# First loads on two DMA queues, biases spread by TensorE, batch 1's first stage from step 2, and matmuls on zeros, in a Fourier and mixture-of-experts kernel

## The chip, the core and the metric

One Trainium2 chip, of which the kernel uses one core. The metric is the device time of one execution in microseconds (us); three runs of the kernel before are given. Engines are named as in the profile: PE is TensorE (matmul), PEld its weight load, DVE VectorE, ACT ScalarE, POOL GpSimd, SP SyncE, which here issues DMAs only.

## The reference

Eight batches of x, each 3136 x 256, float32. Per batch: a real FFT along the 3136 rows, a complex matrix product with w_r + i w_i plus biases, a soft threshold (0.01) on real and imaginary part, and the inverse FFT. On its result `a`, a gate score per row picks 128 rows, which go through a two-layer network and are added back:

```python
X = np.fft.rfft(x, axis=1); Xr, Xi = X.real, X.imag
Yr = Xr @ w_r - Xi @ w_i + b_r
Yi = Xr @ w_i + Xi @ w_r + b_i
Yr = np.sign(Yr) * np.maximum(np.abs(Yr) - 0.01, 0)   # Yi likewise
a = np.fft.irfft(Yr + 1j * Yi, n=3136, axis=1)
scores = np.einsum('bsd,d->bs', a, w_gate)
for b in range(8):
    top = np.argpartition(-scores[b], 128)[:128]
    xe = a[b, top]
    out[b, top] = xe + sigmoid(scores[b, top])[:, None] * (np.maximum(xe @ w1, 0) @ w2)
```

## The kernel before, in words

The transform of 3136 = 98 x 32 rows is done in two stages each way, all as matmuls against tables. Batch by batch:

- **s1** (first stage, 16 units of two columns per batch, U = 16). `ld_x` loads x in tiles of four columns (98 x 1024, 392 KB), eight per batch. For batch 0, `s1` is one float32 matmul per unit on the tile as loaded, against `w1f`. From batch 1 on, `split_x` first splits the tile into a high and a low part (ACT writes `xh`, POOL subtracts for `xl`) and `mm3` makes three matmuls. The result goes from PSUM (four "s" buffers) to SBUF by ACT for even and DVE for odd units, and per two units a tile of 392 KB is stored to a scratch in DRAM, `As`.
- **s2** (13 groups per batch, G = 13). `ld_a` loads `As` back transposed (`av`, 512 KB, two groups per load); four matmuls against `g_sb` give `px` (one PSUM buffer), which ACT, DVE and POOL split into `Xh` and `Xl`.
- **spectral**: 24 matmuls per group with the split weights wrh, wrl, wih, wil into `py`; then DVE adds `bias`, ACT and DVE apply the threshold, and ACT and DVE split into `Yh`, `Yl`.
- **s2i**: six matmuls per group against `gip` (POOL's own queue brings that table in seven pieces); ACT copies the result out, DVE takes the gate's dot product with `wgb`, and it goes to a scratch `Cs`.
- **s1i** and the expert network follow 17 and more steps later and are not touched.

The main loop runs over steps t. In step t stand s2 of group t+1, spectral of group t and s2i of group t-1. Batch 0's first stage stands in the steps before 0; batch 1's has a schedule of its own (lines 595 to 603): loads from t = -2, splits from -1, s1 from 0, spread over ten steps. From batch 2 on it runs 16 steps ahead of the group it serves. `consts_a` (weights and biases) is called before the loop, `consts_g` and `consts_gi` in single steps. The order in which the program's calls reach an engine is settled by a scheduler when it is built; each engine then takes its instructions strictly in that order. `queued` keeps the loads of one queue (`ld` on SP, `ld_r` on POOL) in the order of the program. DMAs of SP and ACT take eight semaphores in turn, so that a DMA isn't issued before the eighth one ahead of it has landed.

Of the kernel before, what the change touches and what calls it, by code (L numbers as in the profile page):

```python
# [10 lines left out]
F32 = mybir.dt.float32  # L11
# [11 lines left out]
NF = 64  # L23
LAM = 0.01
# [84 lines left out]
def fourier_moe(ctx: ExitStack, tc: tile.TileContext, x, w_r, w_i, b_r, b_i, wg, w1, w2,  # L109
# [57 lines left out]
    def consts_a():  # L167
        for src, h, l in ((w_r, wrh, wrl), (w_i, wih, wil)):
            t = pool.tile([128, 2, D], F32, name="r1" if l is wrl else "Yl", bufs=1 if l is wrl else YB)
            ld(t, src.rearrange("(h p) e -> p h e", p=128))  # L170
            nc.vector.tensor_copy(h, t)
            nc.vector.tensor_tensor(out=l, in0=t, in1=h.bitcast(F32), op=ALU.subtract)
        for c, src in enumerate((b_r, b_i)):
            ld(bias[c * NF:(c + 1) * NF], src.rearrange("(o a e) -> o a e", o=1, a=1).broadcast_to([NF, 2, D]))
        nc.vector.tensor_scalar(out=bias, in0=bias, scalar1=LAM, scalar2=None, op0=ALU.add)
        nc.vector.memset(m2l, -2.0 * LAM)
# [5 lines left out]
    def consts_gi(k):  # L182
        s = slice(4 * k, min(4 * k + 4, NJ))
        ld_r(gip[:, s], t_gi[:, s])
        if k == 0:
            ld(wgb, wg.rearrange("(o e) -> o e", o=1).broadcast_to([128, D]))

# [182 lines left out]
    def width(g):  # L370
        return 1 if g == G - 1 else 2

    def ld_x(b, i):
        if i % 2 == 0:
            xt[b, i] = xt[b, i + 1] = pool.tile([N1, 4, D], F32, name=("xt", "cv", "av")[i // 2 // 3] if b == 0 else "xt", bufs=2 if b == 0 and i >= 12 else 3)
            ld(xt[b, i], xv[b, :, 2 * i:2 * i + 4, :])

# [203 lines left out]
    for i in range(U):  # L581
        ld_x(0, i)
    consts_a()
    consts_g(0)
    for t in range(-LEAD, B * G + LAG + 1):
# [3 lines left out]
        if t + LEAD < G or t + LEAD >= 2 * G:  # L589
            at_step(t + LEAD, s1, U)  # L590
        if t == -2:
            ld_x(1, 0)
            consts_g(1)
        at_step(t + AP, ld_a, G)
        for i in range(U):
            if t == -2 + i * 10 // U and i:
                ld_x(1, i)
            if t == -1 + i * 10 // U:
                split_x(1, i)
                if i == 0:  # L600
                    consts_gi(0)
            if t == i * 10 // U:
                s1(1, i)
        if t + LEAD + XP >= 2 * G:
            at_step(t + LEAD + XP, ld_x, U)
# [47 lines left out]
```

## Time and profile before

| | us |
|---|---|
| median of 3 runs (lowest, highest) | 766.38 (764.88, 767.89) |
| the profiled execution's own time | 765.34 |
| its span, first to last instruction | 763.5 |
| PE busy in the span | 727.8 (95%) |
| DVE, ACT, POOL busy | 520.4, 488.3, 356.1 |
| chain that ended last: PE, DVE, DMA | 80%, 9%, 6% |

The span is what the trace shows; the execution's own time has 1.8 us more around it. PE is busy nearly everywhere but in the first 60 us and the last 50. The chain that ended last is read from the end back to what released each piece; its DMA share lies almost wholly at the beginning and at the end.

### The profile page before, as it was taken

Reading aid. Unit: us, or ns where it says so; the run is one execution under the profiler, and the core shown is the slowest. Engines: PE = TensorE matmul, PEld = TensorE weight load, DVE = VectorE, ACT = ScalarE, POOL = GpSimd, SP = SyncE. Lnnn points to the kernel's source line nnn. Section 1 sums busy time; section 2 is a strip of 40 time slices with the busy share of each in tenths; the row PEclk is TensorE's granted clock in tenths of the full one; section 3 lists DMA queues with packets and bytes.
Section 4 is the critical chain, followed back from the end, with each engine's and each line's share of the span. In section 5 each row is a group of like instructions: output and inputs, shape, how many; then the busy total and the mean of one; then the engine's idle time right before and its main releaser. Section 6 shows DMA issues by size and latency. Waiting matters only on the chain.

```text
span 763.5 us, 14877 instructions
## 1 busy us (share of the span) xinstructions
PE 727.8 (95%) x5194; PEld 648.0 (85%) x5194; DVE 520.4 (68%) x1406; ACT 488.3 (64%) x994; POOL 356.1 (47%) x371
## 2 busy tenths in 40 slices
PE   6489999999999999999999999999999999999987
PEld 2279999998999899999998888888999888888657
DVE  2247766666566656655898898676687799887652
ACT  2246666778777767778778768677576565555331
POOL 0154545556666755556455555565453323233011
PEclk9699999999999999999999999999999999999998
DMA  8888958788887887687777778677574374343740
GB/s 225 303 250 270 292 190 279 253 249 277 258 258 236 270 246 250 210 269 242 242 232 234 228 207 263 203 237 215 166 225 146 124 220 140 109 132 113 243 148 22
DMA packets 86650, 165.59 MB, mean 217 GB/s; under 512 B 6413, under 2 KB 59182, under 8 KB 86574
## 3 DMA queue, kind: packets, MB, share of 16 engines
q1 hardware_dynamic: 84302, 158.99, 67.0%
q0 software_dynamic: 2160, 5.60, 2.5%
q8 instruction: 41, 0.67, 0.4%
q14 instruction: 35, 0.29, 0.1%
q10 hardware_dynamic: 112, 0.04, 0.0%
HBM read 86.56 MB, written 78.12 MB: 216 GB/s over the span
## 4 chain that ended last, share of the span: by engine, by line
PE 80%; DVE 9%; DMA 6%; issue 3%; ACT 1%; POOL 0%; SPq 0%; POOLq 0%; ACTq 0%; DVEq 0%
PE py L221 11%; PE py L223 11%; PE py L222 11%; PE px L418 10%; PE s L223 9%; PE s L221 9%; PE s L222 9%; DMA xt<-in_x 2%; PE m L346 2%; DMA As<-at 2%; PE s L501 1%; PE s L393 1%; PE py L346 1%; DVE w L265 1%; DVE Yl L217 1%
## 5 line engine op out<-in xcount | busy, mean ns | idle before, releaser
L217 POOL TENSOR_TENSOR cl<-cv,ch 98x512 fp32r<-98x512 f32 x112 | 144.3, 1290 | 188.0 <-ACT ch L215 131.2
L217 POOL TENSOR_TENSOR xl<-xt,xh 98x512 fp32r<-98x512 f32 x112 | 144.5, 1292 | 126.4 <-ACT xh L215 115.8
L459 ACT COPY ct<-s 128x512 f32<-128x512 f32 (+1 forms) x104 | 59.3, 570 | 164.3 <-PE s L223 150.6
L221 PE MATMUL py<-wrh,Xh 128*128 128x256 f32 x400 | 121.6, 304 | 0.0
L418 PEld LDWEIGHTS px<-g_sb,av 128*128 128x128 f32 (+1 forms) x800 | 106.7, 194 | 13.0 <-DVE Csc L463 1.2
L223 PE MATMUL py<-wrl,Xh 128*128 128x256 f32 x400 | 113.2, 283 | 0.0
L221 PE MATMUL py<-wih,Xh 128*128 128x256 f32 x400 | 113.0, 283 | 0.0
L222 PE MATMUL py<-wih,Xl 128*128 128x256 f32 x400 | 112.9, 282 | 0.0
L223 PE MATMUL py<-wil,Xh 128*128 128x256 f32 x400 | 112.7, 282 | 0.0
L222 PE MATMUL py<-wrh,Xl 128*128 128x256 f32 x400 | 112.7, 282 | 0.0
L463 DVE CUSTOM_DVE_ANT_0 junk<-s,wgb 128x256 f32<-128x256 f32 (+1 forms) x200 | 84.3, 421 | 38.6 <-ACT ct L459 35.3
L418 PE MATMUL px<-g_sb,av 128*128 128x128 f32 (+1 forms) x800 | 109.3, 279 | 0.0
L217 DVE TENSOR_TENSOR Yl<-py,Yh 128x512 fp32r<-128x512 f32 (+1 forms) x104 | 69.3, 666 | 45.4 <-ACT Yh L215 45.4
L438 DVE TENSOR_TENSOR py<-py,bias 128x512 f32<-128x512 f32 (+1 forms) x104 | 70.2, 675 | 42.8 <-PE py L223 42.6
L423 DVE TENSOR_TENSOR Xl<-px,Xh 128x512 fp32r<-128x512 f32 (+1 forms) x104 | 69.2, 666 | 19.6 <-ACT Xh L422 13.2
L215 ACT CAST xh<-xt 98x512 fp32r<-98x512 f32 x112 | 72.3, 651 | 16.0 <-DMA xt<-in_x 14.3
L221 PEld LDWEIGHTS py<-wrh,Xh 128*128 128x128 f32 x400 | 75.7, 189 | 1.6 <-ACT Xh L421 0.6
L440 ACT ACTIVATE r<-py,m2l 128x512 f32<-128x512 f32 (+1 forms) x104 | 70.3, 676 | 10.3 <-DVE py L438 6.0
L221 PEld LDWEIGHTS py<-wih,Xh 128*128 128x128 f32 x400 | 75.3, 188 | 0.9 <-issue 0.9
L223 PEld LDWEIGHTS py<-wrl,Xh 128*128 128x128 f32 x400 | 75.3, 188 | 0.6 <-issue 0.5
L222 PEld LDWEIGHTS py<-wrh,Xl 128*128 128x128 f32 x400 | 75.7, 189 | 0.1
L222 PEld LDWEIGHTS py<-wih,Xl 128*128 128x128 f32 x400 | 75.3, 188 | 0.2 <-issue 0.2
(144 smaller groups left out, 1737.5 us busy)
## 6 DMA issues: line engine op xcount, KB each, us to landing
av<-As SPq DMA_DIRECT2D x48, 512.0 KB
Cs<-ct SPq DMA_DIRECT2D x48, 512.0 KB
As<-at SPq DMA_DIRECT2D x60, 392.0 KB
out<-ot SPq DMA_DIRECT2D x60, 392.0 KB
xt<-in_x SPq DMA_DIRECT2D x59, 392.0 KB
cv<-Cs SPq DMA_DIRECT2D x59, 392.0 KB
gip<-t_gi POOLq DMA_DIRECT2D x6, 512.0 KB, 8.6
out<-at SPq DMA_DIRECT2D x4, 392.0 KB
```

The lines of the kernel that those rows point to most:

```text
L215: nc.scalar.copy(out=h, in_=src)
L217: track[sub] = sub.tensor_tensor(out=l, in0=src, in1=h.bitcast(F32), op=ALU.subtract).ins
L221: nc.tensor.matmul(out, wh, mh, start=start, stop=False)
L222: nc.tensor.matmul(out, wl, mh, start=False, stop=False)
L223: return nc.tensor.matmul(out, wh, ml, start=False, stop=stop).ins
L346: nc.tensor.matmul(ph[:, f, :], w1s[:, h, (4 * q + f) * 128:(4 * q + f + 1) * 128], xT[:, h, :], start=(h == 0), stop=(h == 1))
L418: nc.tensor.matmul(px[:, 2 * p + h, :], a[:, 2 * (g % 2) * (w - 1) + p, h * 128:(h + 1) * 128], g_sb[:r, 2 * g + p, :], start=True, stop=True)
L423: nc.vector.tensor_tensor(out=xl[:, :, NF:], in0=px, in1=xh[:, :, NF:].bitcast(F32), op=ALU.subtract)
L438: nc.vector.tensor_tensor(out=py, in0=py, in1=bias[:, :w, :], op=ALU.add)
L440: nc.scalar.activation(out=r1, in_=py, func=AF.Relu, bias=m2l, scale=1.0)
L459: nc.scalar.copy(out=c, in_=p)
L463: nc.vector.tensor_tensor_reduce(out=junk[:r], in0=c[:, k, :], in1=wgb[:r], scale=1.0, scalar=0.0, op0=ALU.mult, op1=ALU.add, accum_out=Cs ...
```

## The change

- The x tiles of batch 0 with an odd number (units 2, 6 and 10) are loaded from ACT's queue, the other five from SP's as before.
- The biases and the gate vector no longer come as broadcast loads (128 KB each). Three rows of 1 KB are loaded on ACT's queue into `rows`, two matmuls against a selector `sel` spread them over the partitions, and DVE writes `bias` and `wgb` from PSUM.
- `consts_a` and the first `consts_g` are called in step -3, behind batch 0's first stage, no longer before the loop. `wil` is made by POOL, not DVE, and the first piece of `gip` is called right behind it.
- Batch 1: loads from t = 0, splits from 1, s1 from 2, spread over nine steps (before: -2, -1, 0 and ten).
- `warm(n)`: n bf16 matmuls 128 x 512 on a tile of zeros; ten before the loop, 24 in step -3.

```diff
--- before.py
+++ after.py
@@ -169,10 +169,18 @@
             t = pool.tile([128, 2, D], F32, name="r1" if l is wrl else "Yl", bufs=1 if l is wrl else YB)
             ld(t, src.rearrange("(h p) e -> p h e", p=128))
             nc.vector.tensor_copy(h, t)
-            nc.vector.tensor_tensor(out=l, in0=t, in1=h.bitcast(F32), op=ALU.subtract)
-        for c, src in enumerate((b_r, b_i)):
-            ld(bias[c * NF:(c + 1) * NF], src.rearrange("(o a e) -> o a e", o=1, a=1).broadcast_to([NF, 2, D]))
-        nc.vector.tensor_scalar(out=bias, in0=bias, scalar1=LAM, scalar2=None, op0=ALU.add)
+            if l is wil:
+                last[nc.gpsimd] = nc.gpsimd.tensor_tensor(out=l, in0=t, in1=h.bitcast(F32), op=ALU.subtract).ins
+                consts_gi(0)
+            else:
+                nc.vector.tensor_tensor(out=l, in0=t, in1=h.bitcast(F32), op=ALU.subtract)
+        for c in range(2):
+            p = ps.tile([128, D], F32, name="m", bufs=1)
+            nc.tensor.matmul(p, sel[:, c, :], rows, start=True, stop=True)
+            if c == 0:
+                nc.vector.tensor_scalar(out=bias, in0=p.rearrange("p (o e) -> p o e", o=1).broadcast_to([128, 2, D]), scalar1=LAM, scalar2=None, op0=ALU.add)
+            else:
+                nc.vector.tensor_copy(wgb, p)
         nc.vector.memset(m2l, -2.0 * LAM)
 
     def consts_g(k):
@@ -182,8 +190,6 @@
     def consts_gi(k):
         s = slice(4 * k, min(4 * k + 4, NJ))
         ld_r(gip[:, s], t_gi[:, s])
-        if k == 0:
-            ld(wgb, wg.rearrange("(o e) -> o e", o=1).broadcast_to([128, D]))
 
     def consts_b():
         ld_r(w1tp, t_w1t)
@@ -370,10 +376,21 @@
     def width(g):
         return 1 if g == G - 1 else 2
 
+    def warm(n):
+        z = pool.tile([128, D], F32, name="junk", bufs=1)
+        nc.vector.memset(z, 0.0)
+        z = z.bitcast(BF16)
+        p = ps.tile([128, 512], F32, name="m", bufs=1)
+        for _ in range(n):
+            nc.tensor.matmul(p, z[:, :128], z, start=True, stop=True)
+
     def ld_x(b, i):
         if i % 2 == 0:
             xt[b, i] = xt[b, i + 1] = pool.tile([N1, 4, D], F32, name=("xt", "cv", "av")[i // 2 // 3] if b == 0 else "xt", bufs=2 if b == 0 and i >= 12 else 3)
-            ld(xt[b, i], xv[b, :, 2 * i:2 * i + 4, :])
+            if b == 0 and i in (2, 6, 10):
+                nc.scalar.dma_start(out=xt[b, i], in_=xv[b, :, 2 * i:2 * i + 4, :])
+            else:
+                ld(xt[b, i], xv[b, :, 2 * i:2 * i + 4, :])
 
     def split_x(b, i):
         o = 2 * (i % 2)
@@ -580,27 +597,34 @@
 
     for i in range(U):
         ld_x(0, i)
-    consts_a()
-    consts_g(0)
+    rows = pool.tile([65, D], F32, name="hot", bufs=1)
+    sel = pool.tile([65, 2, 128], F32, name="xT", bufs=1)
+    nc.vector.memset(rows, 0.0)
+    nc.vector.memset(sel, 0.0)
+    for c, src in enumerate((b_r, b_i, wg)):
+        nc.vector.memset(sel[32 * c:32 * c + 1, c // 2, (0, NF, 0)[c]:(NF, 128, 128)[c]], 1.0)
+        nc.scalar.dma_start(out=rows[32 * c:32 * c + 1], in_=src.rearrange("(o e) -> o e", o=1))
+    warm(10)
     for t in range(-LEAD, B * G + LAG + 1):
         if t + LEAD + 1 < G or t + LEAD + 1 >= 2 * G:
             at_step(t + LEAD + 1, split_x, U)
         at_step(t - LAG + 1, split_c, U)
         if t + LEAD < G or t + LEAD >= 2 * G:
             at_step(t + LEAD, s1, U)
-        if t == -2:
-            ld_x(1, 0)
-            consts_g(1)
+        if t == -3:
+            consts_a()
+            consts_g(0)
+            warm(24)
         at_step(t + AP, ld_a, G)
         for i in range(U):
-            if t == -2 + i * 10 // U and i:
+            if t == i * 9 // U:
                 ld_x(1, i)
-            if t == -1 + i * 10 // U:
+            if t == 1 + i * 9 // U:
                 split_x(1, i)
-                if i == 0:
-                    consts_gi(0)
-            if t == i * 10 // U:
+            if t == 2 + i * 9 // U:
                 s1(1, i)
+        if t == -1:
+            consts_g(1)
         if t + LEAD + XP >= 2 * G:
             at_step(t + LEAD + XP, ld_x, U)
         at_step(t - LAG + 2, ld_c, U)
```

What the scheduler makes of it, at three places. First SP's queue, from the weights to batch 0's first `av`. Here `r` and `Yl` are the two weights, `As` is the scratch, `xt<-in_x` a tile of batch 1. Before:

```order
L162 DMA r_108<-in_w_r 128x2x256
L162 DMA Yl<-in_w_i 128x2x256
L162 DMA bias<-in_b_r 64x2x256
L162 DMA bias<-in_b_i 64x2x256
L162 DMA g_sb<-t_g 128x512
L401 DMA As<-at 98x1024 x3
L401 DMA As<-ct 98x1024 x2
L401 DMA As<-ot 98x1024 x2
L401 DMA As<-at 98x1024
L162 DMA xt<-in_x 98x1024
L162 DMA g_sb<-t_g 128x512
L162 DMA av<-As 128x4x256
```

With the change:

```order
L162 DMA r_196<-in_w_r 128x2x256
L162 DMA Yl<-in_w_i 128x2x256
L418 DMA As<-at 98x1024 x3
L418 DMA As<-ct 98x1024 x2
L418 DMA As<-ot 98x1024 x2
L418 DMA As<-at 98x1024
L162 DMA g_sb<-t_g 128x512
L162 DMA av<-As 128x4x256
L162 DMA g_sb<-t_g 128x512
L162 DMA av<-As 128x4x256
L162 DMA xt<-in_x 98x1024
```

The biases are gone, the first table and batch 1's first tile stand behind the stores, and the weights still stand ahead of them.

Second DVE, over the same time: copies of batch 0's first stage (`at`, `ct`, `ot`, odd units) and the split of the weights. Before:

```order
L397 COPY at<-s 98x512 x2
L288 COPY row<-nrow 98x1 x2
L397 COPY at<-s 98x512
L397 COPY ct<-s 98x512 x2
L397 COPY ot<-s 98x512
L171 CAST wrh<-r_108 128x512
L397 COPY ot<-s 98x512
L172 TENSOR_TENSOR wrl<-r_108,wrh 128x512
L171 CAST wih<-Yl 128x512
L172 TENSOR_TENSOR wil<-Yl,wih 128x512
L175 TENSOR_SCALAR bias<-bias 128x512
L397 COPY at<-s 98x512 x2
```

With the change:

```order
L414 COPY at<-s 98x512
L294 COPY row<-nrow 98x1 x2
L414 COPY at<-s 98x512 x2
L171 CAST wrh<-r_196 128x512
L176 TENSOR_TENSOR wrl<-r_196,wrh 128x512
L171 CAST wih<-Yl 128x512
L414 COPY ct<-s 98x512 x2
L414 COPY ot<-s 98x512 x2
L414 COPY at<-s 98x512
L181 TENSOR_SCALAR bias<-m 128x512
L183 COPY wgb<-m 128x256
```

The weights' split stood behind the sixth odd unit's copy; now it stands behind the third, ahead of five copies.

Third ACT, where batch 0's second stage begins: `Xh` is the split of a group's `px`, `xh` the split of a unit of batch 1, `r_278` and `r_297` the threshold of group 0. Before:

```order
L215 CAST xh<-xt 98x512 x2
L399 COPY at<-s 98x512
L421 CAST Xh<-px 128x4x128
L422 ACTIVATE Xh<-px 128x4x64
L215 CAST xh<-xt 98x512 x2
L421 CAST Xh<-px 128x4x128
L422 ACTIVATE Xh<-px 128x4x64
L215 CAST xh<-xt 98x512 x2
L399 COPY at<-s 98x512
L440 ACTIVATE r_278<-py,m2l 128x512
L215 CAST xh<-xt 98x512
L421 CAST Xh<-px 128x4x128
```

With the change:

```order
L416 COPY at<-s 98x512
L438 CAST Xh<-px 128x4x128
L439 ACTIVATE Xh<-px 128x4x64
L438 CAST Xh<-px 128x4x128
L439 ACTIVATE Xh<-px 128x4x64
L221 CAST xh<-xt 98x512 x3
L457 ACTIVATE r_297<-py,m2l 128x512
L438 CAST Xh<-px 128x4x128
L439 ACTIVATE Xh<-px 128x4x64
L221 CAST Yh<-py 128x512
```

Of batch 1's splits six stood ahead of group 0's threshold and one more ahead of group 2's `Xh`; now three stand ahead of both. On PE, seven units of batch 1 stood ahead of group 4's `px`; now it is four. Ahead of group 12's `px` there are 19 units in both orders, and from there on the two are the same but for two matmuls.

## Rows read from the trace of the kernel before

**Rows 1.** The page, part 1: the span, and busy time of each engine.

```profile
span 763.5 us, 14877 instructions
PE 727.8 (95%) x5194; PEld 648.0 (85%) x5194; DVE 520.4 (68%) x1406; ACT 488.3 (64%) x994; POOL 356.1 (47%) x371
```

**Rows 2.** Busy time by stretch: us from the span's start, length, busy us and instructions of each engine, then the granted clock of TensorE (1.00 is 2.4 GHz, 0.50 is 1.2 GHz), the busy share of the DMA engines and GB/s.

```profile
4.00:15.00 11.00, 9.21 (x17) 3.54 (x18) 2.31 (x6) 2.34 (x4) 0.00 (x0) 1.00 0.98 251
...
23.00:30.00 7.00, 0.00 (x0) 0.00 (x0) 0.32 (x1) 0.00 (x0) 0.00 (x0) 0.53 0.91 355
30.00:40.00 10.00, 7.09 (x29) 5.14 (x30) 1.29 (x2) 3.99 (x8) 5.48 (x7) 0.65 0.93 239
38.00:41.00 3.00, 2.89 (x23) 2.73 (x24) 0.75 (x2) 1.45 (x4) 2.85 (x3) 1.00 1.36 280
...
49.00:52.00 3.00, 1.99 (x8) 1.65 (x9) 1.90 (x3) 1.40 (x4) 1.50 (x2) 0.78 0.98 318
...
60.00:103.00 43.00, 43.00 (x335) 40.71 (x333) 30.45 (x68) 27.48 (x57) 21.80 (x25) 1.00 0.81 252
```

**Rows 3.** The chain that ended last, in order of time: start, length, what. The beginning, then the `px` matmuls of groups 4, 5, 6 and 12 of batch 0 and of group 0 of batch 1.

```profile
0.73 5.02 DMA w1f<-t_wf
...
14.37 7.51 DMA As<-at
...
23.39 6.13 DMA As<-at
...
38.72 9.32 DMA xt<-in_x
...
59.35 0.90 PE px L418 x8
64.50 0.89 PE px L418 x8
70.32 0.89 PE px L418 x8
...
103.22 0.64 PE px L418 x4
108.33 0.89 PE px L418 x8
```

**Rows 4.** SP's queue in order of time: start, length, what it issues (the length holds its wait, where several are drawn together).

```profile
18.22 1.69 SPq L401 DMA_DIRECT2D As<-ct  x2
...
23.39 0.31 SPq L401 DMA_DIRECT2D As<-at  x1
23.79 0.59 SPq L162 DMA_DIRECT2D xt<-in_x  x1
...
29.59 0.39 SPq L162 DMA_DIRECT2D av<-As  x1
...
93.29 0.31 SPq L401 DMA_DIRECT2D As<-at  x1
99.00 0.38 SPq L162 DMA_DIRECT2D av<-As  x1
```

**Rows 5.** DMA issues by line: what, KB each, and for POOL's queue the us from issue to landing.

```profile
bias<-in_b_r SPq DMA_DIRECT2D x1, 128.0 KB
...
gip<-t_gi POOLq DMA_DIRECT2D x6, 512.0 KB, 8.6
```

**Rows 6.** PE's weight loads of batch 0's first stage, two to a unit: start, length, what, and the idle time before it.

```profile
8.46 0.29 PEld L393 LDWEIGHTS s<-xt,w1f 98*98 98x98 f32 x1 [0.56 <-issue]
9.31 0.29 PEld L393 LDWEIGHTS s<-xt,w1f 98*98 98x98 f32 x1 [0.56 <-issue]
...
20.26 0.17 PEld L393 LDWEIGHTS s<-av,w1f 98*98 98x98 f32 x1 [0.26 <-issue]
20.69 0.17 PEld L393 LDWEIGHTS s<-av,w1f 98*98 98x98 f32 x1 [0.26 <-issue]
```

**Rows 7.** PE's matmuls in order of time: start, length, what. The `px` of groups 0 and 4, and between them two matmuls of a unit of batch 1 at each clock.

```profile
34.25 1.91 PE L418 MATMUL px<-g_sb,av 128*128 128x128 f32 x8
...
51.38 0.63 PE L221 MATMUL s<-xh,w1p 98*98 98x512 f32 x1
51.81 0.63 PE L222 MATMUL s<-xh,w1p 98*98 98x512 f32 x1
...
57.80 0.39 PE L221 MATMUL s<-xh,w1p 98*98 98x512 f32 x1
58.03 0.39 PE L222 MATMUL s<-xh,w1p 98*98 98x512 f32 x1
...
59.20 1.05 PE L418 MATMUL px<-g_sb,av 128*128 128x128 f32 x8
```

**Rows 8.** ACT in order of time: start, length, what, and the idle time before it with what ended it.

```profile
42.34 1.14 ACT L215 CAST xh<-xt 98x512 fp32r<-98x512 f32 x2 [1.72 <-DMA xt<-in_x]
...
48.14 0.62 ACT L215 CAST xh<-xt 98x512 fp32r<-98x512 f32 x1 [3.59 <-DMA xt<-in_x]
...
49.14 0.59 ACT L215 CAST Yh<-py 128x512 fp32r<-128x512 f32 x1
```

**Rows 9.** DVE in order of time: a copy of the first stage and the split of the first weight.

```profile
18.32 0.69 DVE L397 COPY ot<-s 98x512 f32<-98x512 f32 x1 [1.03 <-PE s L393]
18.93 0.42 DVE L171 CAST wrh<-r 128x512 fp32r<-128x512 f32 x1
```

## Prediction

> **What bounds the kernel now.** I read the busy times first, then the stretches, then the chain of waits, and last the queues and engines at the places the chain names. PE works 727.8 of 763.5 us [rows 1], so a change that removes no PE work can only fill holes. From 60 to 103 us there is none: PE is busy 43.00 of 43.00 us at full clock [rows 2]. The holes are at the front, and the chain there is one of DMAs: the constant `w1f` until 5.75, batch 0's first stage, a store that waits behind the loads (14.37 to 21.88), the last store (23.39 to 29.52), then loads of batch 1's x [rows 3]. PE does nothing from 23 to 30, its clock falls to 1.2 GHz (0.53 there, 0.65 from 30 to 40) [rows 2], and group 0's `px` starts at 34.25 [rows 7]. After that ACT, which takes its instructions in order, twice waits for a tile of batch 1 (until 42.34 and 48.14) while group 0's results queue behind it: `Yh` starts 1 us after the second wait [rows 8].
>
> So I follow one path: last store of batch 0 landed, `av`, `px` of group 0, `px` of group 4, `px` of group 12. From there on both programs have the same order on PE, with PE full, so what is won at group 12 should stay. The sum is made against the profiled execution, 765.34 us, which stands 1.04 below the median of 766.38; I add that back at the end. A difference under 0.5% (3.8 us) is no change.
>
> **Term 1: start of group 0's `px`, 34.25 now.** Four edits act on it.
>
> *Bytes ahead of the last store.* The biases (2 x 128 KB [rows 5]) and the first table (256 KB, by the order now behind the stores) leave: 0.52 MB at the 251 GB/s of the first loads [rows 2], 2.1 us less. But two pieces of `gip`, 512 KB each [rows 5], now start behind `wil`, near 20 us, beside the stores on POOL's queue: 1.05 MB at the 355 GB/s of that stretch [rows 2], 2.9 us more if all of it gets ahead of the last store. In exchange they no longer run beside batch 1's loads, one of which took 9.32 us [rows 3].
>
> *Two queues.* Six of the eight tiles (2.4 MB, 9.6 us at 251 GB/s) now come two at a time. No row shows two queues loading x. With POOL's queue and SP's both loading, the DMAs moved 280 GB/s (38 to 41) and 318 (49 to 52) [rows 2]: 8.6 or 7.6 us. I take 8.0, 1.6 us less; bounds 0 and 2.8 (the store rate).
> The Trainium skill's "DMA: Bandwidth & Descriptors", section "Issuing engines are not separate DMA queues", says that DMAs started on several engines share the same 16 DMA engines and save only the issue time. By it this item would be 0; the 280 and 318 against 251 say that something is left, though those loads had other shapes.
>
> *DVE's order.* The weights are not behind the stores: in the order they stand ahead of them, as before, and DVE now splits them ahead of five first-stage copies. Before, the fifth store, which takes the semaphore of `w_i`, was out by 19.9 (18.22 + 1.69 [rows 4]), so `w_i` lands near 19.5; with the faster loads 17.9. Then DVE needs 0.42 for the cast and 0.69 for unit 7's copy [rows 9], and PE, which has four "s" buffers, can't start unit 11 before 19.0. Five units are left. A unit is two rows of 0.43 (0.86 us) at full clock and of 0.86 (1.7 us) at half [rows 6]: PE is done at 23.3, or at 27.6. The last store needs a copy, an issue and about 2.5 us for moving and landing: it lands at 27.5 or 31.8. By bytes it lands at 29.5 - 2.1 + 2.9 - 1.6 = 28.7, so at full clock the stall is hidden, at half it costs 3.
>
> *Zeros.* The ten at the start cost nothing: PE waits for `w1f` until 5.75 [rows 3]. The first units ran at half pitch to past 9.31 [rows 6] (the record has 1.00 there [rows 2]; the pitch tells); if the zeros lift the clock, PE saves about 2 us there, which the loads and DVE take back. The 24 stand behind the bias matmuls and so behind DVE's last copy, about 3 us after the first stage: from 26.2. No row has a bf16 matmul; the nearest, 512 columns too, follow each other in 0.23 us at full and 0.43 at half clock [rows 7]: 5.5 or 10.3 us, ending at 31.7 to 36.5. PE idles enough just ahead of them for a third at half clock: end at 33.3.
>
> `av` is issued as the last store lands, and its `px` began 4.7 us after that issue (29.59 [rows 4], 34.25 [rows 7]); the tile and the table issued from 23.79 on [rows 4] no longer stand ahead of it: I take 4.3. So 28.7 + 0.1 + 4.3 = 33.1 by data, 33.3 by the zeros; half clock in the stall has some weight, and I take **33.9, -0.35**. Bounds: 31.4 (-2.8) and 37.8 (+3.5).
>
> **Term 2: from group 0's `px` to group 4's.** Now 34.25 to 59.20, 24.95 us [rows 7]. ACT and DVE take 0.6 to 0.7 for such tiles [rows 8, 9], `px` 0.89 [rows 3], a matmul 0.12 (the 4.48 of term 3 less 0.89, over 30). With the start as 0, `px` ends at 0.9, `Xl` frees the `px` buffer at 2.2, group 1's `px` ends at 3.1, group 0's spectral at 5.95, group 2's `px` at 6.85, group 1's spectral at 9.7. Group 0's threshold and split are five steps of 0.7 with one `Xh` between them: `Yl` at 9.65, if ACT isn't held. It is held by three `xh`, whose second tile stands 2.3 MB behind the last store: at 30 to 40's 239 GB/s [rows 2] 9.8 us and 1.5 for landing, some 7 after the `px`: 0.9 late. Then s2i, four units of batch 1 between the following groups, `px` of group 3 and one spectral more: **18.3 us, -6.65**. Bounds 17.6 (no hold) and 20 (a second hold as now).
>
> **Term 3: group 4's `px` to group 12's.** The chain gives the step: 5.15 us with one unit of batch 1 (59.35 to 64.50), 5.82 with two (to 70.32), so 4.48 + 0.67 per unit; 8 steps and 12 units make 43.9, and 103.22 - 59.35 is 43.87 [rows 3]. The change leaves 15 units here: **+2.0**.
>
> **Term 4: batch 1's start.** Its last store went out at 93.29 and `av` 5.7 later, at 99.00 [rows 4]; 4.3 more for `av`, against its `px` at 108.2 [rows 3]: 4.9 us of room. One step later (5.82) with the `px` slot 2.2 later leaves 0.9 to 1.3. I charge **+0.3**; bounds 0 and 7.8 (rival C). The DMAs have to carry some 10% more per us between 60 and 100; at a share of 0.81 [rows 2] there is room.
>
> Costed at nothing: the three rows and two bias matmuls (under 1 us, ahead of the zeros), POOL's `wil` (one operation on an engine that has nothing to do then, 0.00 from 4 to 15 and from 23 to 30 [rows 2]), the zero fills on DVE. If POOL's cover is gone, `gip` is later, which only helps the stores.
>
> Sum: -0.35 - 6.65 + 2.0 + 0.3 = -4.7. 765.34 - 4.7 = 760.64, and with 1.04 back **761.7 us**, 0.6% faster.
>
> **Rivals.**
> *A, two queues load no faster* (the skill's rule): `w_i` lands at 19.5, PE idles nearly 4 us, its clock falls as it does in the hole now, and the 24 zeros run largely at half. `px` starts near 36.3: term 1 is +2.1, the sum -2.2, 764.2 us. For it: 251 GB/s at a share of 0.98, so the engines were full. Against: 318 at the same share.
> *B, they load much faster* (bound 2.8) and nothing stalls: term 1 is -2.8, term 2 17.9: 758.8 us. For it: stores of the same tiles run at 355. Against: the 280.
> *C, batch 1 comes too late.* Its first stage ends a step later, and the store and the `av` behind it each take 9.3, like the load at 38.72 [rows 3], for 5.7 and 4.3: group 0 of batch 1 waits 8.6 - 0.9 = 7.7 us, PE stands, and the sum is +2.7, 769.1 us; with A 771.6. It ends slower once the lateness passes 5. For it: DVE and SP queue behind such waits. Against: 4.9 us of room now, and DMAs that are not full.
> *D, it does nothing*: the zeros don't lift the clock and terms 2 and 4 cancel: within 2 us of 766.4. Against: the two holds of ACT must go, since six `xh` leave their place.
>
> **How the numbers follow.** Forecast 0.42 (760 to 763.5), A 0.26, B 0.20, C 0.08, D 0.04. Faster by over 0.5% means below 762.55: 0.7 of the forecast, all of B and a little of A, 0.54. Slower by over 0.5% (above 770.2) is C with A and what I don't see: 0.08. No change: 0.38. The range reaches from below B to C's lower part: 757.8 to 767.5.
>
> **What would show it.** Right: group 0's `px` at 33 to 35 and at 1.00 clock; no stop of ACT at a tile of batch 1 longer than 1 us; group 4's `px` near 52, group 12's near 98.5; batch 1's `px` right behind. Term 1 is wrong if unit 11 starts after 20 us, or if zeros still run when `av` is there. Term 4 is wrong if PE stands just before batch 1's first `px`. The forecast is wrong if group 12's `px` comes after 100.

## The result and the profile after

The change makes the kernel slower: 768.87 us (median of 20 runs, 764.58 to 773.77) against 763.40 (20 runs, 758.78 to 767.94), a ratio of 1.0072, interval 1.0052 to 1.0092. The forecast was 761.7.

The profiled execution took 768.77 us (span 767.0) against 765.34. The stretches of [rows 2], with the place where the clock fell shown by itself (from and to, length, busy us and instructions of PE, PEld, DVE, ACT and POOL, granted clock, DMA share, GB/s):

```profile
4.00:15.00 11.00, 10.04 (x24) 3.77 (x23) 2.47 (x6) 3.53 (x5) 0.00 (x0) 1.00 0.93 271
23.00:30.00 7.00, 5.48 (x26) 2.41 (x25) 1.71 (x3) 0.00 (x0) 0.00 (x0) 1.00 0.93 335
30.00:34.00 4.00, 1.00 (x5) 0.27 (x3) 0.00 (x0) 0.00 (x0) 0.00 (x0) 0.99 0.29 99
34.00:44.00 10.00, 5.73 (x23) 5.17 (x24) 0.78 (x2) 1.86 (x5) 0.40 (x1) 0.50 0.79 239
44.00:54.00 10.00, 10.00 (x81) 9.62 (x80) 6.10 (x13) 6.71 (x14) 6.15 (x7) 0.99 0.71 211
```

The clock stays at 2.4 GHz from 23 to 34, through the zeros and 3 us past them. Then it falls, PE having been busy 1.00 of 4.00 us, and is at 1.2 GHz until 44, so the fall now lies on the first groups' work. The beginning of the chain, with the `px` that answer to [rows 3] (rows left out are marked by dots, here and below):

```profile
1.77 10.36 DMA cv<-in_x
12.15 4.16 DMA r<-in_w_r
...
18.48 3.69 PE s L410 x8
...
24.22 8.81 DMA As<-at
33.17 3.85 DMA av<-As
...
37.16 2.06 PE px L435 x8
...
40.90 2.07 PE px L435 x8
...
57.94 0.90 PE px L435 x8
...
109.35 1.14 PE px L435 x8
```

The last store takes 8.81 us from issue to landing (6.13 in [rows 3]). Group 0's `px` takes 2.06 us at half clock, as it did before (1.91 [rows 7]; at full clock it is 0.89 [rows 3]); but before, the clock was back at full by 38 [rows 2], and now it isn't until 44. PE in order of time (start, length, what, idle time before it and what ended it), beside [rows 6, 7]:

```profile
6.00 2.17 PE L410 MATMUL s<-xt,w1f 98*98 98x512 f32 x4
9.13 3.68 PE L410 MATMUL s<-xt,w1f 98*98 98x512 f32 x8 [0.96 <-DMA xt<-in_x]
12.65 4.45 PE L410 MATMUL s<-cv,w1f 98*98 98x512 f32 x10
18.48 1.10 PE L410 MATMUL s<-cv,w1f 98*98 98x512 f32 x2 [1.38 <-DVE ct L414]
19.41 3.60 PE L410 MATMUL s<-av,w1f 98*98 98x512 f32 x8
...
25.66 5.34 PE L385 MATMUL m<-junk 128*128 128x512 bf16 x24 [0.52 <-DVE wgb L183]
37.16 2.05 PE L435 MATMUL px<-g_sb,av 128*128 128x128 f32 x8 [6.16 <-DMA av<-As]
```

PE loses 0.96 us to the second tile and 1.38 to DVE's copies, is done with batch 0's first stage at 23.0, and stands 6.16 between the zeros and `px`. In the kernel before it was done at 21.7:

```profile
18.11 3.60 PE L393 MATMUL s<-av,w1f 98*98 98x512 f32 x8
```

On POOL (start, length, what), `gip` starts 5 us ahead of the last store's issue:

```profile
17.91 1.27 POOL L173 TENSOR_TENSOR wil<-Yl,wih 128x512 fp32r<-128x512 f32 x1 [14.95 <-DVE wih L171]
19.12 1.17 POOL L165 DMA_DIRECT2D gip<-t_gi  x2
```

### The profile page after: what moved, and what is told of

Its sections match the earlier page's. It is cut to its first block, busy times and chain, and to the rows that moved or that the text cites. A ratio compares the mean times of both kernels' runs of the same rounds, so it can differ in the third digit from the quotient of the medians.

```text
span 767.0 us, 14959 instructions
## 1 busy us (share of the span) xinstructions
PE 737.5 (96%) x5232; PEld 652.1 (85%) x5232; DVE 522.1 (68%) x1413; ACT 488.2 (64%) x994; POOL 357.2 (47%) x372
## 4 chain that ended last, share of the span: by engine, by line
PE 81%; DVE 9%; DMA 5%; issue 3%; ACT 1%; POOL 0%; SPq 0%; POOLq 0%; ACTq 0%; DVEq 0%
PE py L227 11%; PE py L229 11%; PE px L435 11%; PE py L228 11%; PE s L229 9%; PE s L227 9%; PE s L228 9%; PE m L352 2%; PE s L518 2%; DMA cv<-in_x 1%; DMA As<-at 1%; PE py L352 1%; DVE w L271 1%; DVE c L248 1%; DVE junk L480 1%
## 5 line engine op out<-in xcount | busy, mean ns | idle before, releaser
L438 ACT CAST Xh<-px 128x512 fp32r<-128x512 f32 (+1 forms) x104 | 62.0, 597 | 22.2 <-PE px L435 21.3
```

The lines of the kernel that those rows point to most:

```text
L438: nc.scalar.copy(out=xh[:, :, NF:], in_=px)
```

## The experiments

Each median is that of 11 or 12 runs (20 in the first two rows, six for 52 zeros); the kernel before stood at 763.9 to 764.7 in the same comparisons, and the ratio is to it. Two kernels a few tenths of a per cent apart, with intervals that overlap, are not told apart by these runs. The last columns are each kernel's one profile, in us: start of group 0's `px`, from there to group 4's, on to group 12's, on to batch 1's first. "Front" is the two queues, the biases by PE, the zeros and the weights' new place; its `gip` starts with the weights' split.

| kernel | median | ratio [95%] | g0 | to g4 | to g12 | to batch 1 |
|---|---|---|---|---|---|---|
| before | 763.40 | 1 | 34.25 | 24.9 | 44.0 | 5.0 |
| the change | 768.87 | 1.0072 [1.0052, 1.0092] | 37.16 | 20.6 | 46.1 | 5.5 |
| e1: gip later | 765.04 | 1.0011 [0.9983, 1.0039] | 32.45 | 20.2 | 46.3 | 5.7 |
| e2: before, gip at the stores | 759.88 | 0.9938 [0.9911, 0.9964] | 36.31 | 19.6 | 44.0 | 5.0 |
| e3: 52 zeros | 773.42 | 1.0118 [1.0076, 1.0160] | 36.42 | 24.5 | 46.1 | 7.2 |
| e4: batch 1 as before | 765.78 | 1.0025 [0.9997, 1.0053] | 37.89 | 21.2 | 44.0 | 5.0 |
| e5: e1 and e4 | 767.25 | 1.0047 [1.0012, 1.0082] | 37.63 | 20.2 | 44.3 | 5.0 |
| e6: e4 without the 24 zeros | 762.33 | 0.9975 [0.9949, 1.0001] | 36.74 | 18.8 | 44.0 | 5.0 |
| e7: e4, one queue | 762.60 | 0.9982 [0.9950, 1.0015] | 34.18 | 20.5 | 44.0 | 5.0 |
| e8: e7, no zeros at all | 762.29 | 0.9975 [0.9944, 1.0005] | 35.42 | 22.1 | 44.0 | 5.0 |
| f1: the change, one queue | 762.46 | 0.9971 [0.9941, 1.0000] | 29.22 | 21.0 | 46.1 | 6.2 |
| f2: the change without the 24 zeros | 765.62 | 1.0026 [0.9996, 1.0056] | 35.91 | 21.8 | 46.1 | 5.9 |
| f3: f1, gip later | 761.32 | 0.9963 [0.9934, 0.9992] | 30.30 | 19.7 | 46.3 | 6.0 |
| f4: e2, batch 1 late | 764.32 | 0.9997 [0.9968, 1.0027] | 33.13 | 20.9 | 46.1 | 5.9 |
| g1: two queues, weights behind | 764.54 | 1.0014 [0.9990, 1.0037] | 31.24 | 20.6 | 46.6 | 6.4 |
| g2: f1, gip early | 766.57 | 1.0024 [0.9996, 1.0053] | 31.40 | 21.3 | 46.3 | 5.8 |
| g3: f1, batch 1 between | 762.52 | 0.9981 [0.9952, 1.0010] | 29.25 | 23.5 | 44.7 | 5.0 |
| g4: e2, batch 1 between | 761.96 | 0.9971 [0.9951, 0.9991] | 34.52 | 21.3 | 44.7 | 5.0 |

### Where gip starts

e1 takes `gip` away from the stores; the call behind `wil` goes:

```diff
+        if t == -2:
+            gate = pool.tile([128, 1], F32, name="gate", bufs=1)
+            last[nc.gpsimd] = nc.gpsimd.tensor_copy(gate, av[0, 0][:, 0, :1]).ins
+            consts_gi(0)
```

> The changed kernel, but gip's two pieces start only when the av of batch 0 that follows the last store has landed (a one-column copy on POOL of that tile stands ahead of them). Theory 1 (gip's megabyte drains beside batch 0's stores, holds the last one back to 33.0 us, so px of group 0 comes 6.2 us after the zeros and the clock falls from 33.9 to 44.1): last store lands at 28.5 to 29.5, px of group 0 starts at 32.7 to 33.5 (37.16 with the change), group 4's px at 51 to 53 (57.78), and the time is 5 to 6 us under the changed kernel's, 0.2 to 0.8% under that of the kernel before unless gip, now late, holds the spectral of group 0 up. Rival a (the stores are held by the order of the weights, by DVE or by ACT's queue): last store still at 32 to 33, px at 36 to 37, time as with the change, 0.5 to 0.9% over before. Rival b (the clock's fall near 34 comes whatever PE does): px at 33 but group 1's px still 4 us behind it, and only 3 us won.

SP's queue in e1 (start, length, what): the last store and the first `av` behind its landing.

```profile
23.67 0.31 SPq L417 DMA_DIRECT2D As<-at  x1
24.03 1.01 SPq L162 DMA_DIRECT2D g_sb<-t_g  x1
28.44 0.38 SPq L162 DMA_DIRECT2D av<-As  x1
```

The store lands after 4.6 us instead of 8.81, `px` starts at 32.45, and the kernel is 3.8 us faster. Theory 1 holds for the store; the time fell short of its 5 to 6 us, and its last clause, under the kernel before, did not come. g2 is the reverse, in the kernel with one queue (f1, below): `gip` early by a copy that waits for unit 13, nothing else.

```diff
+        if (b, i) == (0, 13):
+            gate = pool.tile([N1, 1], F32, name="gate", bufs=1)
+            last[nc.gpsimd] = nc.gpsimd.tensor_copy(gate, at[b][:, o, :1]).ins
+            consts_gi(0)
+            consts_gi(1)
```

> The changed kernel with one queue (weights behind the stores by themselves) and gip's two pieces started near 19 us, as in the change, by a copy on POOL that waits for unit 13's result. Theory 1 (gip beside the stores holds the last store by 2 to 4.5 us): last store issued near 20.5 but landed at 27.5 to 29.5 (25.1 with one queue and gip late), px of group 0 at 31.5 to 33.5 (29.22), group 4's px at 51 to 53; what gip no longer takes from batch 1's tiles gives part of it back: 762 to 765 us. Rival (gip only fills gaps): last store landed by 26, px of group 0 by 30, and 759.5 to 762 us.

POOL and SP in g2:

```profile
18.48 1.16 POOL L165 DMA_DIRECT2D gip<-t_gi  x2
```

```profile
20.12 0.31 SPq L414 DMA_DIRECT2D As<-at  x1
...
27.35 0.37 SPq L162 DMA_DIRECT2D av<-As  x1
```

The store takes 7.1 us from issue to landing against 4.9 in f1, `px` is 2.2 later, and the kernel 4.1 us slower. The store landed just ahead of the stretch that I gave, and the time was worse.

In the kernel before a move of `gip` to the stores helps. e2 has this edit, and `consts_gi(0)` leaves batch 1's first split:

```diff
-            nc.vector.tensor_tensor(out=l, in0=t, in1=h.bitcast(F32), op=ALU.subtract)
+            if l is wil:
+                last[nc.gpsimd] = nc.gpsimd.tensor_tensor(out=l, in0=t, in1=h.bitcast(F32), op=ALU.subtract).ins
+                consts_gi(0)
+            else:
+                nc.vector.tensor_tensor(out=l, in0=t, in1=h.bitcast(F32), op=ALU.subtract)
```

> The kernel before with one edit of the change: the split of wil on POOL, and gip's two pieces behind it, near 20 us, instead of at batch 1's first split. Theory 1: the last store of batch 0 lands 3 to 4 us later than the 29.5 of before, px of group 0 at 37 to 38 (34.25 before), but less waiting of ACT for batch 1's tiles later, since gip is no longer beside them (groups 1 to 4 win back 1 to 3): time 0 to 0.5% over before. Rival a (gip's place costs the stores nothing): px of group 0 at 34 to 34.5, and the time 0.1 to 0.4% under before.

`px` of group 0 was 2.1 later, in theory 1's direction but short of its 2.8 to 3.8. Groups 0 to 4 won back 5.3, well over the 1 to 3 that I gave them, and so the kernel is 4 us faster than before, where theory 1 had it the same or slower. The edit did less than the expectation above says. POOL in e2:

```profile
23.05 0.63 POOL L165 DMA_DIRECT2D gip<-t_gi  x1
34.03 2.50 POOL L221 TENSOR_TENSOR xl<-xt,xh 98x512 fp32r<-98x512 f32 x2 [10.35 <-ACT xh L219]
36.48 0.57 POOL L165 DMA_DIRECT2D gip<-t_gi  x1
```

Only the first of `gip`'s two pieces moved (33.17 before); the second stands behind batch 1's first splits on POOL, as it did before (35.04). It is the same in e4 and e6, which have batch 1's steps of before: 37.25 and 36.91. In the change and in f4 and g4 (below) both pieces start together. With the first piece off batch 1's loads, ACT's longest wait for a tile between 36 and 52 us is 1.15, where it had 1.72 and 3.59 [rows 8]. With batch 1's old steps and both pieces late it is 1.80 to 4.19 (second profile of the kernel before, e5, e7, e8), with the first piece early 1.40 at most (e2, e4, e6). **So with batch 1's old steps those long waits came from `gip` beside batch 1's loads**, and moving its first piece alone shortens them. e5 has it the other way round (the edits of e1 and e4 together):

> Both edits together: the changed kernel with gip behind the first av, and with batch 1's loads, splits and first stage at the steps of before. Theory 1 (two separate losses that add: gip beside batch 0's stores holds px of group 0 back by 4 us, and batch 1's later schedule costs 2 to 3 us on its own): px of group 0 at 32.5 to 34, group 4's px at 53 to 54.5, group 12's 43.9 behind it or less, batch 1's px 5.0 behind that: 761.5 to 763 us, 0.2 to 0.5% under before. Rival d (gip then lands beside batch 1's loads, as in the kernel before, and ACT is held by its tiles again): group 4's px 24 to 25 behind group 0's, and 764 to 766 us.

It fell out above the times of theory 1 and rival d alike: `gip` late meets batch 1's early loads again, and units of batch 1 stand ahead of `px` on PE. Moving `gip` and moving batch 1 are two remedies for one collision. On the change's front, both give 768.9, `gip` alone 765.8 (e4, its first piece only), batch 1 alone 765.0 (e1), none 767.3 (e5). Beyond the noise, the change is slower than e1 and e4; e5's interval overlaps with those of all three.

### The second queue

f1 loads all eight tiles on SP's queue:

```diff
-            if b == 0 and i in (2, 6, 10):
-                nc.scalar.dma_start(out=xt[b, i], in_=xv[b, :, 2 * i:2 * i + 4, :])
-            else:
-                ld(xt[b, i], xv[b, :, 2 * i:2 * i + 4, :])
+            ld(xt[b, i], xv[b, :, 2 * i:2 * i + 4, :])
```

> The changed kernel with all first loads on SP's queue and nothing else undone; the weights' loads then stand behind the stores in SP's order, and their splits behind DVE's first-stage copies. Theory 2 (moving three loads to ACT's queue is the largest loss of the change: it puts the weights ahead of the stores): last store issued at 20 to 20.5 (24.22 with the change), av at 25.5 to 26.5 (33.17), px of group 0 at 30 to 33, 4 to 6 us under the changed kernel, 763 to 765. Rival (gip beside the stores holds px whatever the queue): px at 35 to 37, 767 to 769.

It is 6.4 us faster than the change, a little more than theory 2 gave. In f1's order SP's weights stand behind the stores; with them DVE's splits and `gip` go back. SP, PE and POOL in f1:

```profile
20.20 0.31 SPq L415 DMA_DIRECT2D As<-at  x1
20.56 0.40 SPq L162 DMA_DIRECT2D r<-in_w_r  x1
...
25.24 0.37 SPq L162 DMA_DIRECT2D av<-As  x1
```

```profile
22.00 6.98 PE L385 MATMUL m<-junk 128*128 128x512 bf16 x24 [0.52 <-DVE wgb L183]
29.22 1.13 PE L432 MATMUL px<-g_sb,av 128*128 128x128 f32 x8 [0.24 <-DMA av<-As]
...
32.04 1.98 PE L432 MATMUL px<-g_sb,av 128*128 128x128 f32 x8 [0.63 <-DVE Xl L437]
```

```profile
28.61 1.17 POOL L165 DMA_DIRECT2D gip<-t_gi  x2
```

Here the zeros end 0.24 us ahead of `px`, which starts at full clock; group 1's `px`, 3 us later, runs at half all the same. g1 parts the order from the queue: two queues, but the weights' loads ordered behind the last store.

```diff
-            nc.sync.dma_start(out=As[b][:, 2 * i - 2:2 * i + 2, :], in_=at[b])
+            st = nc.sync.dma_start(out=As[b][:, 2 * i - 2:2 * i + 2, :], in_=at[b]).ins
+            if (b, i) == (0, U - 1):
+                last[nc.sync] = st
```

> The changed kernel, two queues kept, with the weights' loads ordered behind batch 0's last store on SP, which puts their splits behind DVE's first-stage copies and gip's start behind the stores. Theory 2a (the order costs, not the second queue): PE does not wait for DVE's copies, last store issued at 20 to 21.5 (24.22 with the change), av at 25 to 26.5, px of group 0 at 29 to 31, 761.5 to 764 us. Rival 2b (the second queue itself costs: ACT is blocked behind its own loads, and two tiles in flight land later than one): last store issued at 22.5 or later, px of group 0 at 32 or later, 765 to 769 us.

The result lies between the two. The order brings 4.3 us, probably most of it by `gip`, which starts at 30.65 here: e1 won 3.8 with the weights still ahead. The second queue itself costs 2 us against f1, by the medians and by the start of `px`; the ratios differ by 0.43%, just beyond their noise. PE in g1:

```profile
5.60 1.88 PE L410 MATMUL s<-xt,w1f 98*98 98x512 f32 x4
9.31 3.68 PE L410 MATMUL s<-xt,w1f 98*98 98x512 f32 x8 [1.83 <-DMA xt<-in_x]
```

The first tiles are under way together, and the second lands when PE has waited 1.83 us for it; in f1 PE never waits there.

e7 and e8 are f1's edit on e4, e8 also without `warm(10)` and `warm(24)`; f3 is f1 with e1's edit.

> The changed kernel with batch 1's steps as before, and all first loads on SP's queue. The weights' loads now stand behind the stores in SP's order. Theory g (two queues load at 271 instead of 251 GB/s, worth about 0.7 us of 9.6): px of group 0 0.5 to 1 us later than 37.9, time 766 to 767. Rival h (the order counts, not the number of queues: with the weights behind the stores neither PE waits for DVE's copies nor the loads for semaphores of ACT's queue): the first stage ends 1 to 2 us earlier, px of group 0 at 35 to 36.5, time 762 to 764.5.

The time is rival h's; group 0's `px` came even earlier than it had.

> The changed kernel with batch 1's steps as before, no zeros at all and all first loads on SP's queue: beside the kernel before, only gip's place, the biases by PE and the place of the weights are changed. The kernel before with gip's place alone ran in 759.9. Theory i (two queues and zeros are what costs the other 5.9 us): 758.5 to 761. Rival j (the biases by PE and the weights behind the first stage cost it): 764 to 767.

It is neither: with one queue the zeros, which end 5 us ahead of `px` in e7, are worth nothing either way (762.6 and 762.3). What e8 still lacks against e2 is 2.4 us, within the noise of the two; its late `gip` lies beside batch 1's tile, which took 15.24 us, so that may be the reason, but no run shows it.

> The changed kernel with all first loads on SP's queue and gip started only when the first av has landed. Theory 2 with theory 1 (both losses of the front gone): last store issued at 20 to 20.5, av at 25 to 25.5, px of group 0 at 29.2 to 30 with the zeros ending at 29.2 and so no fall of the clock there, group 4's px at 49 to 50.5; batch 1's later schedule still costs its 2.6: 758 to 761 us, 0.4 to 0.8% under before. Rival (the next transfer takes over, as with gip late and batch 1 early): group 4's px past 53, and 763 or more.

Theory 2 with theory 1 nearly holds: the clock stays at 1.00 from 7 us to 703, yet groups 0 to 4 take 19.7, since ACT waits for batch 1's tiles (1.99, 1.84 and 1.71 us).

### The zeros

> The changed kernel with 52 zero matmuls instead of 24 between the first stage and group 0. At 0.21 to 0.23 us each they end at 37 to 37.6, as px of group 0 could start at 37.16. Theory 1 with the clock (of what the change lost, some 2.3 us are px and spectral at 1.2 GHz in a hole of 6.2 us that the zeros did not cover): the clock stays at 1.00 from 26 on, px of group 0 at 37.2 to 37.8 and group 4's px at 55.5 to 56 (57.78): 1.5 to 2.3 us under the changed kernel, and still 0.3 to 0.6% over before. Rival b (the clock's fall does not hang on the hole): same clock rows, and the time as with the change or 0.5 us over it.

The edit is `warm(52)` for `warm(24)`. Both missed: the kernel is 4.5 us slower, by something that neither had. With more zeros the scheduler arrives at another order and puts three splits of batch 1 ahead of group 0's. ACT in e3, with `px` of group 0 at 36.42:

```profile
40.07 1.14 ACT L221 CAST xh<-xt 98x512 fp32r<-98x512 f32 x2 [17.76 <-DMA xt<-in_x]
42.01 0.62 ACT L221 CAST xh<-xt 98x512 fp32r<-98x512 f32 x1 [0.80 <-DMA xt<-in_x]
42.53 0.58 ACT L438 CAST Xh<-px 128x512 fp32r<-128x512 f32 x1
```

e6 and f2 leave `warm(24)` out, of e4 and of the change.

> The changed kernel with batch 1's steps as before, and without the 24 zeros ahead of group 0. Theory e (the zeros take nothing from the chain and keep the clock up only until 34.9, so they are worth little): px of group 0 within 1 us of the 37.9 that it had with the zeros, the clock falls near 24 instead of 34.9 and is back near 41 instead of 45: time within 2 us of that kernel's 765.8. Rival f (the zeros make the clock fall in the spectral work instead of in the wait for the stores, and so cost time): group 4's px 1.5 to 3 us earlier, 762.5 to 764.

e6 is 3.4 us faster than e4, a little more than rival f said. The clock by stretches (columns as above), e4 and then e6:

```profile
30.00:35.00 5.00, 1.71 (x8) 0.74 (x7) 0.00 (x0) 0.92 (x2) 0.21 (x1) 0.99 0.97 295
35.00:40.00 5.00, 4.74 (x14) 2.75 (x13) 0.69 (x1) 0.96 (x3) 2.83 (x3) 0.50 0.90 228
40.00:45.00 5.00, 4.31 (x16) 3.79 (x17) 0.69 (x1) 2.55 (x6) 2.90 (x3) 0.50 0.89 267
```

```profile
30.00:35.00 5.00, 0.57 (x2) 0.40 (x2) 0.00 (x0) 1.14 (x2) 0.54 (x1) 0.50 0.92 281
35.00:40.00 5.00, 4.62 (x18) 3.21 (x16) 0.81 (x2) 2.53 (x5) 3.77 (x4) 0.65 1.03 275
40.00:45.00 5.00, 5.00 (x40) 4.67 (x41) 1.66 (x3) 2.64 (x6) 4.83 (x6) 1.00 0.98 319
```

With the zeros PE waits at full clock and works at half. Without them it waits at half, and its clock is back at full within 2 us of the `px` at 36.74, 7 us earlier than with them.

> The changed kernel without the 24 zeros ahead of group 0. Theory 3 (the zeros move the clock's fall from the wait for the stores, where it is free, to the first groups, where it costs): the clock is back at 1.00 by 38 to 40 instead of 44.1, px of group 0 at 36 to 37.5, group 4's px at 54.5 to 56.5 (57.78), time 2 to 4 us under the changed kernel. Rival (zeros are neutral): same px of group 4, time within 1 us of the changed kernel.

f2 is 3.2 us faster than the change in the runs; its profile does not show where: its `px` of group 12 is at 103.80 (103.87 with the zeros), and its clock was down from 28.5 to 45.6. Only the time agrees with theory 3.

### Batch 1's steps

e4 puts the lines of the old schedule back (loads -2, splits -1, s1 0, ten steps).

> The changed kernel with batch 1's loads, splits and first stage at the steps they had before. Theory 1 (the loss is at the front, batch 1's later schedule gave 4.3 us in groups 0 to 4 and cost 2.1 in groups 4 to 12 and 0.5 at batch 1's start): px of group 0 at 37.2 again, group 4's px 24 to 25 us behind it instead of 20.6, group 12's 43.9 behind that: 1.5 to 2 us over the changed kernel, 0.9 to 1.2% over before. Rival c (the later schedule is what costs): px of group 12 at 101 to 102, time 0.2 to 0.6% under the changed kernel.

My theory was wrong here, and rival c right in time: e4 is 3.1 us faster than the change, though group 12's `px` stands at 103.05, past its 101 to 102. f4 adds the late steps (nine, from 0, 1 and 2) to e2; g3 and g4 have loads from -1, splits from 0, s1 from 1, nine steps, on f1 and on e2.

> The kernel before with gip behind wil's split on POOL (759.9 us alone) and batch 1's loads, splits and first stage at the later steps of the change; the front otherwise as before. Theory 4 (the waits of ACT for batch 1's tiles came from gip beside those tiles, so the later schedule has nothing left to win in groups 0 to 4, and costs 2.1 us in groups 4 to 12 and up to 1 at batch 1's start): px of group 0 at 35 to 36.5, group 4's px 19.5 to 20.6 behind it, 761.5 to 763.5 us. Rival (my forecast's term 2: without units of batch 1 between them the first groups run in 18.3): group 4's px 18 to 18.8 behind group 0's, and 758 to 760 us.

> The changed kernel with one queue and batch 1's loads, splits and first stage one step earlier than the change has them (still nine steps, so the last unit stands at the step of before). Theory 4 (late units of batch 1 cost in groups 4 to 12 and at batch 1's start): group 0 to group 4 as with one queue (21) or 1 longer, 43.9 to 45.5 from group 4's px to group 12's, 5.0 to 5.5 to batch 1's first px (6.2): 759.5 to 761.5 us against 762.5. Rival (batch 1's tiles then stand ahead of the first groups' data again): group 4's px past 52.5, and 762.5 to 765 us.

> The kernel before with gip behind wil's split on POOL, and batch 1's steps between those of before and those of the change. With the steps of before it ran in 759.9, with those of the change in 764.3. Theory 4: between the two, 761 to 763 us. Rival (most of the price is the last step, batch 1's start behind its DMAs): 759 to 760.5 us.

On e2 two steps later cost 4.4 us, with the step between in the middle: 759.9, 762.0, 764.3 (in theory 4's direction; f4 ends 0.8 above my stretch, and its `px` of group 0 came at 33.13, ahead of it). `gip`'s second piece moved with them, from 36.48 to 23.8 and 23.4, so what the steps cost by themselves is not parted from that; the same holds for e4 against the change. On one queue, where both pieces stay late, the steps cost nothing: 762.6, 762.5, 762.5, and g3 came out as its rival had it, with group 4's `px` at 52.71 and ACT waiting for batch 1's tiles.

Late steps cost 2.1 to 2.6 us from group 4 to 12 and 0.5 to 2.2 at batch 1's start in every profile. They also give back, in a place that the column "to g4" doesn't show: with the early steps units of batch 1 stand ahead of group 0's own `px` on PE. From the first `av`'s issue to that `px` it is 7.2 us in e4 and 8.6 in e7, but 4.0 in the change and in f1. Counted from the program's start, group 4's `px` comes earlier with the late steps in all four pairs: 57.78 for 59.09 (the change, e4), 52.67 for 57.79 (e1, e5), 50.21 for 54.66 (f1, e7) and 53.98 for 55.95 (f4, e2). At batch 1's first `px` two of the four are still ahead (e1 by 2.4, f1 by 1.1) and two behind (the change by 1.3, f4 by 1.0). That is less loss than the runs show for e4 and e2; in the profiles the rest lies at the end of the program.

### The end of the program

> The changed kernel once more, unchanged, for a second profile. Over the profiles so far the last batch's end (from the px of its group 11) took 82.1 to 88.4 us, longer with more time at 1.2 GHz. If that is a matter of the single execution, this profile's end differs by 1 us or more from the 86.3 of the first and px of group 0 stands at 36 to 38 again; if the change sets it, it is 86.0 to 86.6 again.

> The kernel before once more, for a second profile. If the end is a matter of the single execution it differs by 1 us or more from 84.2; if the program sets it, it is 83.9 to 84.5 again, and px of group 0 at 33.5 to 35 and of group 4 at 58 to 60 in either case.

Nothing is edited in these two. From group 11 of the last batch to the end the change took 86.3 and 85.9 us, the kernel before 84.2 and 81.7, with the same order there. Before, first and second profile:

```profile
700.00:714.00 14.00, 13.42 (x66) 8.40 (x65) 7.04 (x23) 5.08 (x11) 3.62 (x4) 0.88 0.72 212
```

```profile
700.00:714.00 14.00, 13.51 (x80) 9.52 (x79) 7.94 (x28) 5.12 (x12) 3.74 (x4) 1.00 0.71 223
```

At 0.88 PE does 66 matmuls, at 1.00 it does 80. So 2.5 us there are a matter of the single execution. The change's second end, 0.4 off its first, meets neither sign that I gave. And chance may not be all: ten profiles with late steps have an end of 83.7 to 88.4, mean 86.2, ten with earlier steps 81.7 to 85.1, mean 83.6. The clock is at half for 10.2 us of that end on average with late steps and for 6.6 with earlier ones, which goes with the longer ends but does not say where it comes from: from 117 us on, every engine has the same operations in the same order in the kernel before and in the change. I know no cause for that; it stays open.

## Why the prediction was wrong

In short: with the second queue the weights stay ahead of the stores, their split starts `gip` beside the last store of batch 0, and that store lands at 33.0 where I had it at 28.7. One queue alone undoes the whole loss (f1). A further 2 to 4 us lie at the end of the program, where the sum had nothing; their cause stays open.

**Term 1 failed.** Group 0's `px` was to start at 33.9 and started at 37.16 (37.50 in the second profile). The step that failed is the price of the last store. I let it land at the later of two times, 28.7 by bytes and 27.5 by the chain of PE, copy and issue. In the runs the transfer beside it came on top of the chain. PE was done at 23.0 (forecast 23.3) and the store issued at 24.22; with `gip` later it takes 4.6 to 5.0 us (e1, f1, f3, e8, g1), not my "about 2.5", so the chain alone gives 28.3 (e1: 28.29). `gip` then puts 2.2 to 4.2 us on top (g2; the change against e1). In the second profile of the change the clock was at half from 19.4 to 22.9, behind a stall of 1.73: PE was done only at 25.5, and the store, issued at 26.35, took 7.0. The bytes that I had taken off, 2.1 for the biases and 1.6 for two queues, are not seen in PE's times: it was done 1.3 us later than before (23.0 for 21.7), having waited for a tile and for DVE's copies.

**The item "two queues" failed in sign.** I took 1.6 us of gain; it cost about 2 (g1 against f1), besides the order that comes with it. The Trainium skill's "DMA: Bandwidth & Descriptors", section "Issuing engines are not separate DMA queues", had it: the engines behind the queues are shared. The traces agree that a second queue adds no bandwidth: from 4 to 15 us the nine profiles with two queues show 255 to 277 GB/s, the six of the same front with one queue 239 to 306. Rival A drew on that and came nearest in reason, but neither its time (764.2) nor its mechanism is what happened: unit 11 started at 18.48, by the 19.0 of the text.

**"DVE's order"** was read rightly, and called hidden at full clock. The stall was 1.38 us. That `gip` starts behind `wil` was read as well: near 20, and it was 19.12. But its 2.9 us stood on the byte side alone, where the 3.7 taken off for the biases and the second queue hid them; the chain had none of it.

**The zeros** ended at 31.0 (forecast 33.3), 6.16 us ahead of `px`, because the term's other end was late. I had allowed for half clock in the stall, not for a fall on the groups.

**Term 2** gave 20.6 (21.6 in the second profile) for a forecast of 18.3; a good half of the gain came. The misses are `px` and the spectral matmuls at half clock (2.06 for 0.89), and the reason. I had the gain come from batch 1's steps; e2 has it with the move of one piece of `gip` alone (19.6), and f4, with the late steps besides, has no more (20.9). No kernel with late steps ran below 19.7, even at full clock (f3).

**Term 3** was right: 46.09 for 43.95, +2.1 against +2.0. **Term 4** was +0.5 in the first profile and +1.8 in the second, against +0.3, inside its bounds; with the last unit at the step of before it is nothing (g3, g4).

**"What is won at group 12 should stay"** is a term put at nothing, and it failed too. The first pair of profiles adds up to +2.9 - 4.3 + 2.1 + 0.5 + 0.2 up to the last batch's group 11, and 2.1 at the end: 3.5 us of span. The second pair has 3.9 up to that group and 4.2 at the end, 8.1 in all. The runs have 5.5. So the end makes half of the loss that the profiles show or more, though the order there is the same; why, no run shows.

Undone singly, the parts give back 6.4 (f1), 3.8 (e1), 3.2 (f2) and 3.1 (e4): they overlap and don't add.

**The better version** is e2, the kernel before with `gip`'s first piece behind POOL's split of `wil` and nothing else of the change: 759.88 us, 0.6% under the kernel before and 1.2% under the change.

## What to carry to other kernels

A transfer started beside the last link of a chain was paid on top of that link here (2.2 to 4.2 us); don't take the later of "by bytes" and "by chain" unasked, and look what else an earlier load sets off. When a change brings two remedies, look whether both cure the same wait, since each has its own price. Filler matmuls are not free. In these runs they never paid: with two queues, where they ended early and the clock fell on the work instead of on the wait, leaving them out won 3.2 and 3.4 us; with one queue it changed nothing; and more of them, up to the work's own start, cost 4.5 through the order. After an edit of a call's place, read in the trace which instructions moved: in e2 only one of two pieces did.

## What was not expected of the hardware

- The same loads by the same instructions ran at 239 GB/s (f3) and 306 (f1), at a DMA share of 0.92 and 0.91. So one profile of a front bound by loads does not tell 2 us apart: `px` of group 0 stood at 34.25 and 32.27 in two profiles of the kernel before, and its batch 1 began at 108.17 and 108.33 all the same.
- Added work can cost through the order and not by itself: with 28 more zeros `px` of group 0 came 0.7 us earlier (36.42 for 37.16), but ACT had three splits of batch 1 first, and the kernel was 4.5 us slower.
